# Reordering two places of a linear-attention and gated-FFN kernel: the matmuls of one of seven products, with the VectorE work around them, and the first copies of x

## Chip, cores and metric

The kernel runs on one core of a Trainium2 chip. The metric is device time in microseconds (us) of one execution; lower is better. The engines are called PE (TensorE; PEld is its loading of the stationary operand), DVE (VectorE), ACT (ScalarE), POOL (GpSimd) and SP (SyncE, which issues the DMAs).

## The reference

The input x is 2048 rows of 576. Everything is float32.

```python
xn = layernorm(x)
q, k, v = split(xn @ wqkv)                  # 32 heads of 18
pq, pk = phi(q), phi(k)                     # phi(t) = where(t > 0, t + 1, exp(t)) + 1e-6
s = ((pq @ (pk.T @ v)) / (pq . sum(pk) + 1e-6)) @ wo   # by head
h = gelu(xn @ w1 + b1)                      # 576 -> 4608
g = silu(h @ w2 + b2)                       # 4608 -> 576
out = x + s * g
```

## The kernel before

**Arithmetic.** Every float32 operand of a matmul is split into two parts that PE takes at full rate: hi is a rounded copy (made by ACT), lo is what is left, source minus hi (made by DVE; a few by POOL). A product is then three matmuls: hi by hi, hi by lo, lo by hi. A hi part of h is made at line 673, a lo part at line 676; the lo subtraction of h reads two operands from SBUF.

**Stages.** The first stage loops over 16 tiles of 128 rows: layernorm, transpose into xh and xl (lines 204 to 220), projections to k and v, and the state k.T @ v. The second stage makes q and s. The third is the FFN, whose first product (line 1119) starts at 312.4 us of the span; most of the change is there.

**The FFN.** Its loop (line 1346) has 18 steps: two halves of the rows, each with 9 chunks of four 128-wide tiles of the 4608. A step has two parts. First, two "Up" blocks (one for each pair of tiles) form xn @ w1 by a scheme of seven block products instead of eight, in the order UP = (1, 6, 7, 5, 2, 3, 4); DVE adds the products up in PSUM (lines 1009 to 1026), and ACT makes four g tiles of 128x512 by gelu (line 997) in each Up. Second, seven products (ORDER = (1, 2, 7, 4, 5, 3, 6)) form h @ w2 by the same kind of scheme. Each is done in two halves, q2 = 0 and q2 = 2; a half has two row tiles q of 128 and a PSUM bank for each, and six matmuls for each q: three for pair 0, three for pair 1 (line 1119). DVE then adds the half into the accumulator macc (line 1126). I write product (i, q2), and hi(i, pair) and lo(i, pair) for the parts of h that product i uses. CHAIN = {2: 1, 3: 5, 4: 7} says that product 2 goes on adding into the PSUM banks of product 1, 4 into those of 7, and 3 into those of 5: so PE can't start product (2, 0) before DVE has read product (1, 0) into macc, nor (4, 0) before DVE has read (7, 0).

The sources of product 1 are the g tiles as they come: (1, 0) from the first Up, (1, 1) from the second. Those of 7, 5, 6 and 3 are differences and sums that POOL makes in place (method S, lines 1073 to 1088): S(7, pair) writes the tile mid (line 1088), S(5, pair) is line 1079, S(6, pair) line 1082, S(3, pair) line 1085. S(6, 0) overwrites the source of lo(1, 0), so POOL waits for that.

**Order of the work.** The order of instructions on DVE, ACT, POOL and PE is the program's own (in_order, line 57). A step has 28 places: 0 to 6 after the products of the first Up, 7 to 13 after those of the second, 14 + 2k and 15 + 2k after the two halves of the k-th product. At each place the table PH (line 1314) issues S, hi and lo work. Places are counted after the product's own DVE and ACT work: place 11 stands behind the gelu of product 2 of the second Up and before the DVE addition of its product 3 (line 1022); place 12 behind that addition and before that of product 4 (line 1026); place 13 behind that one. Place 14 stands behind the macc addition of product (1, 0), place 15 behind that of (1, 2). The lines of PH before:

```python
lo={
    (1, 0): 10, (2, 0): 10, (1, 1): 11, (2, 1): 13, (7, 0): 14, (7, 1): 15, (4, 0): 16,
```

**The beginning.** For the first row tile (t = 0) the transposed x lies in PSUM. DVE copies k-blocks 0 and 1 to xh (line 212), ACT blocks 2 to 4 (line 213); then DVE subtracts for xl in two parts (line 217) and for the last 64 rows (line 218). The weights of k are split as they land: hi by ACT (line 260), lo by DVE or POOL (line 263). The lo parts of k-blocks 3 and 4 are both issued inside layernorm(1) (function last_lo), between its statistics and its normalization (line 186).

Of the kernel before, what the change touches and what calls it, by code (L numbers as in the profile page):

```python
# [18 lines left out]
HD = 288  # L19
# [5 lines left out]
KT = 5  # L25
# [17 lines left out]
def linear_attention_gated_ffn(ctx, tc, x, wqkv, wo, w1, w1e, b1, w2, b2, out):  # L43
    nc = tc.nc
# [35 lines left out]
    def bank2(name):  # L80
        return psum.tile([P, 2, 512], F32, tag="pp", name=name)
# [23 lines left out]
    xh, xl = {}, {}  # L105
# [52 lines left out]
    wk_h = wkvp.tile([P, KT, D], F32R, name="wk_h")  # L158
    wk_l = wkvp.tile([P, KT, D], F32R, name="wk_l")
# [5 lines left out]
    def load_x(t):  # L165
        xraw[t] = (
            stw.tile([P, D], F32, tag="stw", name=f"x{t}") if t < 2 else stage(D, f"x{t}")
        )
        nc.sync.dma_start(xraw[t], x[t * P : (t + 1) * P, :])
# [3 lines left out]
    def layernorm(t, between=lambda: None):  # L173
        st = t1.tile([P, 2, 6], F32, tag="st", name=f"st{t}")
        nc.vector.bn_stats(st[:, 0, :], xraw[t][:, :HD])
        nc.vector.bn_stats(st[:, 1, :], xraw[t][:, HD:])
        mv = t1.tile([P, 4], F32, tag="mv", name=f"mv{t}")
        nc.vector.bn_aggr(mv[:, 0:2], st)
        nc.vector.tensor_scalar_add(mv[:, 2:3], mv[:, 1:2], 1e-5)
        nc.gpsimd.tensor_tensor(mv[:, 3:4], mv[:, 2:3], nhalf, op=ALU.pow)  # L180
        stats[t] = mv
        between()
        if t < 2:
            xn[t] = t1.tile([P, 640], F32, tag="xn", name=f"xn{t}")
            for dst, src in norm_parts(t):
                nc.vector.tensor_scalar(dst, src, mv[:, 0:1], mv[:, 3:4], op0=SUB, op1=MUL)
# [8 lines left out]
    def norm_parts(t):  # L195
        return (xn[t][:, :D], xraw[t]), (xn[t][:, D:], xraw[t][:, 512:])
# [7 lines left out]
    def transpose_x(t):  # L204
        pt = bank2(f"pt{t}").rearrange("p a b -> p (a b)")
        for k in range(KT):
            nc.tensor.transpose(pt[:, k * P : (k + 1) * P], xn[t][:, k * P : (k + 1) * P], ident)
        b, c = divmod(t, 4)
        cs = slice(c * P, (c + 1) * P)
        p3 = pt[:, : KT * P].rearrange("p (k c) -> p k c", k=KT)  # L210
        if t == 0:
            nc.vector.tensor_copy(xh[b][:, :2, cs], p3[:, :2])
            nc.scalar.copy(xh[b][:, 2:, cs], p3[:, 2:])
        else:
            nc.scalar.copy(xh[b][:, :, cs], p3)  # L215
        for k in (slice(0, 2), slice(2, 4)) if t == 0 else (slice(0, 4),):
            nc.vector.tensor_tensor(xl[b][:, k, cs], p3[:, k], xh[b][:, k, cs].bitcast(F32), op=SUB)  # L217
        nc.vector.tensor_tensor(
            xh[b][64:, 4, cs], p3[64:, 4, :], xh[b][64:, 4, cs].bitcast(F32), op=SUB
        )  # L220
# [30 lines left out]
    def load_w_raw(which, k):  # L251
        if which == 2:
            raw = raw_places[k]
        else:
            raw = stage(D, f"w{which}_{k}")
        nc.sync.dma_start(raw, wqkv[k, :, which * D : (which + 1) * D])
        return raw

    def w_hi(raw, k, hi):
        nc.scalar.copy(hi[:, k, :], raw)  # L260

    def w_lo(raw, k, hi, lo, elo):
        elo.tensor_tensor(lo[:, k, :], raw, hi[:, k, :].bitcast(F32), op=SUB)

    def split_w(raw, k, hi, lo, elo):
        w_hi(raw, k, hi)
        w_lo(raw, k, hi, lo, elo)


    warm = bank1("warm")  # L270
# [159 lines left out]
    raw_k = [load_w_raw(1, k) for k in range(KT)]  # L430
    load_x(1)
    layernorm(0, lambda: split_w(raw_k[0], 0, wk_h, wk_l, nc.vector))
    split_w(raw_k[1], 1, wk_h, wk_l, nc.gpsimd)
    transpose_x(0)
    split_w(raw_k[2], 2, wk_h, wk_l, nc.gpsimd)
    for k in (3, 4):
        w_hi(raw_k[k], k, wk_h)

    def last_lo():
        for k in (3, 4):  # L440
            w_lo(raw_k[k], k, wk_h, wk_l, nc.vector)

    raw_v = [load_w_raw(2, k) for k in range(KT)]
    load_x(2)
    layernorm(1, last_lo)
    pend = None
    WQ_LOADS = {11: (0,), 12: (1, 2), 13: (3, 4)}
    WQ_SPLITS = {13: (0,), 14: (1, 2), 15: (3, 4)}
# [5 lines left out]
    for t in range(NT):  # L454
# [12 lines left out]
        if t + 1 < NT:  # L467
            if t + 1 in (8, 12):
                x_block((t + 1) // 4)
            transpose_x(t + 1)  # L470
# [225 lines left out]
    class W1:  # L696
# [39 lines left out]
        def product(self, i):  # L736

            r = we_sb[self.n][:, WE_AT[i]]
            if i == 6:
                t = self.tiles[6] if self.n < NP else six[self.n]  # L740
                return t[:, :2], t[:, 2:], r
            key, k = {1: "a0", 2: "a1", 7: "c0", 3: "c1", 5: "d0", 4: "d1"}[i]
            t, k = self.tiles[key], 2 * int(k)
            return t[:, k : k + 2], t[:, 4 + k : 6 + k], r
# [361 lines left out]
    CHAIN = {2: 1, 3: 5, 4: 7}  # L1106
    DST = {1: U1, 2: C11, 5: C22, 3: C12, 6: U1, 7: C22, 4: C21}

    def product(c, i, q2, hs, w, held):

        wh, wl = w
        ps = held.pop((CHAIN[i], q2)) if i in CHAIN else bank2(f"pm{i}")
        if i in CHAIN.values():
            held[i, q2] = ps
        for q in range(2):
            cs = slice((q2 + q) * P, (q2 + q + 1) * P)
            seq = [(st, m, p) for p in range(2) for st, m in ((0, wh), (0, wl), (1, wh))]
            for n, (st, m, p) in enumerate(seq):
                nc.tensor.matmul(  # L1119
                    ps[:, q, :HD], hs[p][st][:, cs], m[:, p, :],  # L1120
                    start=(n == 0 and i not in CHAIN), stop=(n == len(seq) - 1),
                    skip_group_check=True,
                )
        src, dst = ps[:, :, :HD], macc[:, q2 : q2 + 2, DST[i], :]
        if c > 0 or i in (5, 6):
            nc.vector.tensor_tensor(dst, src, dst, op=ADD)  # L1126
        elif i in BIAS:
            h = BIAS[i]
            bb = b2b[:, None, h * HD : (h + 1) * HD].to_broadcast([P, 2, HD])
            nc.vector.tensor_tensor(dst, src, bb, op=ADD)  # L1130
        else:
            nc.vector.tensor_copy(dst, src)
# [160 lines left out]
    def plan_w1(add, w, base, T, hi, lo):  # L1293
        for table, what in ((T, w.T), (hi, w.hi), (lo, w.lo)):
# [5 lines left out]
        hi={"a": 0, 6: 2, "c": 3, "d": 4},  # L1300
        lo={"a": 0, 6: 3, "c": 4, "d": 5},
# [3 lines left out]
        hi={"a": 6, 6: 25, "c": 26, "d": 27},  # L1305
        lo={"a": 7, 6: 25, "c": 26, "d": 27},
# [9 lines left out]
        hi={  # L1316
            (1, 0): 7, (2, 0): 9, (7, 0): 10, (1, 1): 11, (2, 1): 12, (7, 1): 15, (4, 0): 16,
            (4, 1): 17, (5, 1): 18, (5, 0): 19, (6, 0): 20, (3, 0): 21, (3, 1): 22, (6, 1): 23,
        },
        lo={  # L1320
            (1, 0): 10, (2, 0): 10, (1, 1): 11, (2, 1): 13, (7, 0): 14, (7, 1): 15, (4, 0): 16,
            (4, 1): 17, (5, 1): 18, (5, 0): 19, (6, 0): 20, (3, 0): 21, (3, 1): 22, (6, 1): 23,
        },
    )
# [18 lines left out]
    seq = ExitStack()  # L1343
    seq.enter_context(in_order(nc.vector.engine, nc.scalar.engine, nc.gpsimd.engine, nc.tensor.engine))
    n_chunks = 2 * NC
    for step in range(n_chunks):
# [78 lines left out]
        for j in range(CF // 2):  # L1425
            n = 2 * step + j
# [8 lines left out]
        for k, i in enumerate(ORDER):  # L1435
            for q2 in (0, 2):
                product(c, i, q2, [h.ops[i, 0], h.ops[i, 1]], w2t[step].ops[i], held)
                at_step(base + 14 + 2 * k + q2 // 2)
# [47 lines left out]
```

## Time and profile before

| what | value |
|---|---|
| median of 3 runs | 1125.4 us (1124.8 to 1125.44) |
| profiled execution | 1125.94 us, of which the span 1124.2 us |
| granted PE clock, mean | 0.999 |
| PE busy | 1103.8 us (98%) |
| DVE busy | 795.4 us (71%) |
| ACT busy, POOL busy | 452.4 us (40%), 451.3 us (40%) |
| time of DMA packets | 68.7% of 16 engines |

A line of the timeline reads: start, duration, engine, source line, operation, output <- input, shapes, count (consecutive like instructions are merged), and in brackets the idle time of the engine before it with what ended it. A line of the waits reads: who waited for whom, total us, times, longest us. Since matmuls are pipelined, a PE that is called busy may still lose time; the distance between starts shows it.

### The profile page before, as it was taken

The page shows a single profiled execution, that of the slowest core. Times are in us where ns is not written, and L with a number is a line of the kernel's source. Part 1 is how long each engine was busy: PE and PEld are TensorE (multiplying, and loading weights), DVE is VectorE, ACT ScalarE, POOL GpSimd, SP SyncE. Part 2 cuts the span into 40 slices and gives each one's busy share as a digit, 9 for nine tenths or more (in the row PEclk, how much of TensorE's full clock was granted, in tenths as well). Part 3 has the DMA queues.
Part 4 walks back from the last instruction along what each step waited for, and adds up shares of the span by engine and source line. Part 5 has one row for each costly group of instructions (what it writes and reads, how often), then busy time and mean ns, then how long its engine had stood idle before and what let it go on. Part 6 is the DMA issues. An engine that isn't in the chain of part 4 may idle for free. (4 is left out here: it accounts for less than half of the span.)

```text
span 1124.2 us, 18622 instructions
## 1 busy us (share of the span) xinstructions
PE 1103.8 (98%) x6972; PEld 1018.5 (91%) x6972; DVE 795.4 (71%) x1160; ACT 452.4 (40%) x772; POOL 451.3 (40%) x391
## 2 busy tenths in 40 slices
PE   8999999999999999999999999999999999999997
PEld 8999989999898988988989889898898988989987
DVE  6665448989687887877868878667475574765766
ACT  4554443333535444354443544524223242242342
POOL 4976423333344353353534523415234143242340
PEclk9999999999999999999999999999999999999999
DMA  8796832474877659467585589997777677776452
GB/s 324 264 370 254 300 137 72 160 257 157 296 248 270 239 179 342 171 242 266 181 328 193 205 302 343 315 344 242 254 233 213 206 219 215 235 211 208 131 184 85
DMA packets 84968, 264.03 MB, mean 235 GB/s; under 512 B 10381, under 2 KB 20877, under 8 KB 81295
## 3 DMA queue, kind: packets, MB, share of 16 engines
q1 hardware_dynamic: 84879, 262.85, 68.7%
q8 instruction: 55, 0.90, 0.3%
q14 instruction: 34, 0.28, 0.1%
HBM read 166.69 MB, written 94.18 MB: 232 GB/s over the span
## 5 line engine op out<-in xcount | busy, mean ns | idle before, releaser
L676 DVE TENSOR_TENSOR h_l<-g,h_h 128x512 fp32r<-128x512 f32 x204 | 174.8, 864 | 37.0 <-ACT h_h L673 21.3
L1126 DVE TENSOR_TENSOR macc<-pm,macc 128x576 f32<-128x576 f32 x218 | 163.7, 751 | 43.0 <-PE pm L1119 42.1
L673 ACT CAST h_h<-g 128x512 fp32r<-128x512 f32 x204 | 120.8, 620 | 138.1 <-PE pm L1119 137.0
L1088 POOL TENSOR_TENSOR mid<-g 128x512 f32<-128x512 f32 x34 | 43.7, 1285 | 141.0 <-ACT g L997 141.0
L1082 POOL TENSOR_TENSOR g<-g 128x512 f32<-128x512 f32 x34 | 55.1, 1621 | 56.2 <-DVE h_l L676 54.9
L997 ACT ACTIVATE g<-b,b1c 128x512 f32<-128x512 f32 x36 | 24.7, 687 | 115.8 <-DVE b L1015 115.8
L1006 ACT COPY mid<-a 128x512 f32<-128x512 f32 x36 | 21.1, 587 | 117.3 <-PE a L989 117.3
L717 POOL TENSOR_TENSOR w1raw<-w1raw 128x256 f32<-128x256 f32 x18 | 16.9, 938 | 122.5 <-DVE wa L733 122.5
L1214 POOL TENSOR_TENSOR fin1l<-fin1h,fin1l 128x288 f32<-128x288 f32 x8 | 6.5, 807 | 126.3 <-DMA fin1l<-s_dram 51.1
L1009 DVE TENSOR_TENSOR mid<-b,mid 128x512 f32<-128x512 f32 x36 | 24.7, 687 | 44.6 <-PE b L989 43.0
L1079 POOL TENSOR_TENSOR g<-g 128x512 f32<-128x512 f32 x34 | 52.2, 1535 | 2.7
L1085 POOL TENSOR_TENSOR g<-g 128x512 f32<-128x512 f32 x34 | 49.7, 1461 | 2.7
L989 PE MATMUL a<-h0r,wa 128*128 128x512 f32 x144 | 50.4, 390 | 0.0
L989 PE MATMUL a<-xh,wa 128*128 128x512 f32 x144 | 50.4, 390 | 0.0
L997 ACT ACTIVATE g<-e,b1c 128x512 f32<-128x512 f32 x36 | 24.8, 690 | 55.8 <-DVE e L1022 55.8
L1015 DVE TENSOR_TENSOR b<-e,mid 128x512 f32<-128x512 f32 x36 | 25.2, 699 | 30.3 <-PE e L989 30.3
L614 POOL TENSOR_TENSOR pbuf<-phiq,den 128x576 f32<-128x576 f32 x16 | 20.4, 1273 | 63.9 <-DVE den L613 45.1
L217 DVE TENSOR_TENSOR xl<-pt,xh 128x512 fp32r<-128x512 f32 (+1 forms) x17 | 11.1, 660 | 47.9 <-ACT xh L215 47.3
L1012 DVE TENSOR_TENSOR mid<-zy,mid 128x512 f32<-128x512 f32 x36 | 24.9, 691 | 24.6 <-PE zy L989 24.6
L311 POOL TENSOR_TENSOR w2r<-w2r 128x576 f32<-128x576 f32 x27 | 38.8, 1442 | 6.5 <-DMA w2r<-w 5.8
L1022 DVE TENSOR_TENSOR e<-e,mid 128x512 f32<-128x512 f32 x36 | 24.9, 691 | 19.8 <-PE e L989 19.8
L676 DVE TENSOR_TENSOR h_l<-mid,h_h 128x512 fp32r<-128x512 f32 x34 | 38.6, 1134 | 0.0
(810 smaller groups left out, 3617.0 us busy)
## 6 DMA issues: line engine op xcount, KB each, us to landing
we<-we_dram SPq DMA_DIRECT2D x72, 224.0 KB
op<-w2o SPq DMA_DIRECT2D x27, 576.0 KB
w2raw<-w SPq DMA_DIRECT2D x10, 1152.0 KB
w2r<-w SPq DMA_DIRECT2D x9, 1152.0 KB
w1raw<-w SPq DMA_DIRECT2D x18, 512.0 KB
op_a<-wa SPq DMA_DIRECT2D x18, 512.0 KB
op_c<-wc SPq DMA_DIRECT2D x18, 512.0 KB
op_d<-wd SPq DMA_DIRECT2D x18, 512.0 KB
```

The source lines that it names most:

```text
L311: nc.gpsimd.tensor_tensor(dst, a, b, op=SUB)
L673: nc.scalar.copy(pair[0], src)
L676: eng.tensor_tensor(pair[1], src, pair[0].bitcast(F32), op=SUB)
L989: nc.tensor.matmul(ps, st, mv, start=first and n == 0, stop=n == len(seq) - 1, skip_group_check=True,)
L997: nc.scalar.activation(g, ps, AF.Gelu_apprx_tanh, bias=b1c[:, f : f + 1])
L1012: tt(u2_sb, Z, u1_sb, op=ADD)
L1015: tt(B, E, u2_sb, op=ADD)
L1079: tt(src[5, pr], A(1, 0), A(1, 1), op=ADD)
L1082: tt(src[6, pr], src[5, pr], A(0, 0), op=SUB)
L1085: tt(src[3, pr], A(0, 1), src[6, pr], op=SUB)
L1088: tt(src[7, pr], A(0, 0), A(1, 0), op=SUB)
L1126: nc.vector.tensor_tensor(dst, src, dst, op=ADD)
```

## The change

Three edits.

1. In product 1 the matmuls that use lo(1, 1), the last of the six of each q, are issued after the other ten of the half: q = 0 numbers 0 to 4, q = 1 numbers 0 to 4, then number 5 of both. All other products keep their order.
2. In PH, lo(7, 0) goes from place 14 to place 11 and lo(1, 1) from 11 to 12. DVE's order was lo(1, 0), lo(2, 0), lo(1, 1), addition of line 1022, addition of line 1026, lo(2, 1), macc (1, 0), lo(7, 0), macc (1, 2); it becomes lo(1, 0), lo(2, 0), lo(7, 0), line 1022, lo(1, 1), line 1026, lo(2, 1), macc (1, 0), macc (1, 2).
3. At the beginning, DVE makes both copies of the first tile of x, each just ahead of the subtraction that uses it, and ACT none; the lo of k-block 3 of wk is issued ahead of layernorm(1) instead of inside it.

```diff
-        if t == 0:
-            nc.vector.tensor_copy(xh[b][:, :2, cs], p3[:, :2])
-            nc.scalar.copy(xh[b][:, 2:, cs], p3[:, 2:])
-        else:
+        if t:
             nc.scalar.copy(xh[b][:, :, cs], p3)
-        for k in (slice(0, 2), slice(2, 4)) if t == 0 else (slice(0, 4),):
+        for k, n in ((0, 2), (2, 4)) if t == 0 else ((0, 4),):
+            k, kh = slice(k, n), slice(k, KT if n == 4 else n)
+            if t == 0:
+                nc.vector.tensor_copy(xh[b][:, kh, cs], p3[:, kh])
             nc.vector.tensor_tensor(xl[b][:, k, cs], p3[:, k], xh[b][:, k, cs].bitcast(F32), op=SUB)
...
-    for k in (3, 4):
-        w_hi(raw_k[k], k, wk_h)
-
-    def last_lo():
-        for k in (3, 4):
-            w_lo(raw_k[k], k, wk_h, wk_l, nc.vector)
-
+    split_w(raw_k[3], 3, wk_h, wk_l, nc.vector)
     raw_v = [load_w_raw(2, k) for k in range(KT)]
     load_x(2)
-    layernorm(1, last_lo)
+    layernorm(1, lambda: split_w(raw_k[4], 4, wk_h, wk_l, nc.vector))
...
-        for q in range(2):
+        seq = [(st, m, p) for p in range(2) for st, m in ((0, wh), (0, wl), (1, wh))]
+        seq = [(q, n, *s) for q in range(2) for n, s in enumerate(seq)]
+        if i == 1:
+
+            seq.sort(key=lambda s: s[1] == 5)
+        for q, n, st, m, p in seq:
             cs = slice((q2 + q) * P, (q2 + q + 1) * P)
-            seq = [(st, m, p) for p in range(2) for st, m in ((0, wh), (0, wl), (1, wh))]
-            for n, (st, m, p) in enumerate(seq):
-                nc.tensor.matmul(
-                    ps[:, q, :HD], hs[p][st][:, cs], m[:, p, :],
-                    start=(n == 0 and i not in CHAIN), stop=(n == len(seq) - 1),
-                    skip_group_check=True,
-                )
+            nc.tensor.matmul(
+                ps[:, q, :HD], hs[p][st][:, cs], m[:, p, :],
+                start=(n == 0 and i not in CHAIN), stop=(n == 5), skip_group_check=True,
+            )
...
         lo={
-            (1, 0): 10, (2, 0): 10, (1, 1): 11, (2, 1): 13, (7, 0): 14, (7, 1): 15, (4, 0): 16,
+            (1, 0): 10, (2, 0): 10, (7, 0): 11, (1, 1): 12, (2, 1): 13, (7, 1): 15, (4, 0): 16,
```

The rest of the diff merges the helpers w_hi and w_lo into split_w.

More of the change, by code (lines that the diff above doesn't have):

```diff
@@ L257, in load_w_raw, with split_w @@
         return raw
-    def w_hi(raw, k, hi):
+    def split_w(raw, k, hi, lo, elo):
         nc.scalar.copy(hi[:, k, :], raw)
-    def w_lo(raw, k, hi, lo, elo):
         elo.tensor_tensor(lo[:, k, :], raw, hi[:, k, :].bitcast(F32), op=SUB)
-    def split_w(raw, k, hi, lo, elo):
-        w_hi(raw, k, hi)
-        w_lo(raw, k, hi, lo, elo)
     warm = bank1("warm")
```

## The prediction

> **What bounds the kernel now.** I read the shares of the engines first, then the waits, then the timeline of one FFN step, engine by engine.
>
> ```profile
> PE 1103.8 (98%) x6972; PEld 1018.5 (91%) x6972; DVE 795.4 (71%) x1160; ACT 452.4 (40%) x772; POOL 451.3 (40%) x391
> ```
>
> PE is the bound, so only two things can move the time: the number of matmuls, which stays the same, and the places where PE loses time between them. The waits name such a place:
>
> ```profile
> PE pm L1119 <- DVE macc L1126: 7.8, 15, 0.6
> ```
>
> Matmuls of h @ w2 wait for the macc addition, 15 times (two more, in the steps where macc is first written, go by another line: 17 steps have products). How much is lost in all, I take from the step's length, since pipelining hides part of a wait. From the chain that ended last, products without a gap and one product of the Up part:
>
> ```profile
> 1057.50 13.03 PE pm L1119 x96
> ...
> 1080.10 1.59 PE zy L989 x7
> ```
>
> 96 matmuls are eight halves of 12: about 1.60 us each (13.03 less some 0.2 us of the last one's tail, by 8). A step has 14 Up products and 14 halves: 14 x 1.59 + 14 x 1.60 = 44.7 us of work. Its real length is the distance of two equal DVE rows, 812.66 - 766.76 = 45.90 us:
>
> ```profile
> 766.76 0.70 DVE L1015 TENSOR_TENSOR b<-e,mid 128x512 f32<-128x512 f32 x1 [0.90 <-PE e L989]
> ...
> 812.66 0.70 DVE L1015 TENSOR_TENSOR b<-e,mid 128x512 f32<-128x512 f32 x1 [0.90 <-PE e L989]
> 813.27 1.28 DVE L676 TENSOR_TENSOR h_l<-g,h_h 128x512 fp32r<-128x512 f32 x2
> 815.93 1.70 DVE L676 TENSOR_TENSOR h_l<-g,h_h 128x512 fp32r<-128x512 f32 x1 [1.38 <-POOL g L1082]
> 817.55 0.69 DVE L1022 TENSOR_TENSOR e<-e,mid 128x512 f32<-128x512 f32 x1
> 818.15 0.68 DVE L1026 TENSOR_TENSOR zy<-zy,mid 128x512 f32<-128x512 f32 x1
> 819.71 0.69 DVE L676 TENSOR_TENSOR h_l<-g,h_h 128x512 fp32r<-128x512 f32 x1 [0.87 <-issue]
> 820.31 0.75 DVE L1126 TENSOR_TENSOR macc<-pm,macc 128x576 f32<-128x576 f32 x1
> 820.98 1.12 DVE L676 TENSOR_TENSOR h_l<-mid,h_h 128x512 fp32r<-128x512 f32 x1
> 822.03 0.75 DVE L1126 TENSOR_TENSOR macc<-pm,macc 128x576 f32<-128x576 f32 x1
> 822.69 1.12 DVE L676 TENSOR_TENSOR h_l<-mid,h_h 128x512 fp32r<-128x512 f32 x1
> ...
> 827.16 0.74 DVE L1126 TENSOR_TENSOR macc<-pm,macc 128x576 f32<-128x576 f32 x1
> ```
>
> So **a step loses 45.90 - 44.66 = 1.24 us, and 17 steps lose 21.1 us**, 1.9% of the time. PE's own timeline shows where:
>
> ```profile
> 815.41 0.39 PE L989 MATMUL e<-rxm,we 128*128 128x512 f32 x1
> ...
> 817.22 0.42 PE L1119 MATMUL pm<-w__8548,h_h 128*128 128x288 f32 x2
> ...
> 820.27 0.29 PE L1119 MATMUL pm<-w__8548,h_l 128*128 128x288 f32 x1
> 821.12 0.53 PE L1119 MATMUL pm<-w__8586,h_h 128*128 128x288 f32 x2 [0.55 <-DVE macc L1126]
> ...
> 828.01 0.50 PE L1119 MATMUL pm<-w__8660,h_h 128*128 128x288 f32 x2
> ```
>
> Product 1 runs from 817.22 without a gap; product (2, 0) should start at 820.40 (a matmul each 0.133 us) and starts at 821.12, right after the macc of (1, 0), in whose banks it goes on, ends at 821.06. Two halves of (2) and two of (7) later, (4, 0) starts at 828.01, after the macc of (7, 0) ends at 827.90, though 4 x 1.60 after 821.12 is 827.5: the rest of the loss.
>
> Why is the macc of (1, 0) late? Its matmuls ended by 818.9, but DVE came to it at 820.31. Backwards: lo(2, 1) waited until 819.71 for its hi; that stood behind the gelu that follows the addition of line 1022; this addition ran at 817.55, although its last matmul (the 815.41 row) ended at 815.80. In between DVE stood in lo(1, 1): 1.70 us instead of the 0.69 of the 819.71 row. POOL's timeline says why:
>
> ```profile
> 807.87 1.29 POOL L1088 TENSOR_TENSOR mid<-g 128x512 f32<-128x512 f32 x1 [4.27 <-ACT g L997]
> ...
> 814.10 1.61 POOL L1082 TENSOR_TENSOR g<-g 128x512 f32<-128x512 f32 x1 [3.56 <-DVE h_l L676]
> ...
> 815.79 1.29 POOL L1085 TENSOR_TENSOR g<-g 128x512 f32<-128x512 f32 x1
> ...
> 820.28 1.27 POOL L1088 TENSOR_TENSOR mid<-g 128x512 f32<-128x512 f32 x1 [3.20 <-ACT g L997]
> 821.64 1.63 POOL L1079 TENSOR_TENSOR g<-g 128x512 f32<-128x512 f32 x1
> 823.34 1.64 POOL L1082 TENSOR_TENSOR g<-g 128x512 f32<-128x512 f32 x1
> ```
>
> A lo part that meets a running POOL sum ends 0.55 us after that sum: 817.63 after S(3, 0) ended at 817.08, 822.10 after 821.55, 823.81 after 823.27. And a sum that meets a lo part takes 1.16 us from its end (823.81 to 824.98). The two exclude each other. The macc additions, which read PSUM, are not held up (0.75 us at 822.03, under a POOL sum). Where both wait, DVE's subtraction goes ahead of POOL's next sum (823.27, 823.34, 823.81).
>
> **The change part by part.** *Edit 2, lo(7, 0) earlier.* I replay the step of 812.66 with these durations. ACT's rows are:
>
> ```profile
> 813.98 0.61 ACT L673 CAST h_h<-mid 128x512 fp32r<-128x512 f32 x1
> ...
> 815.22 0.62 ACT L673 CAST h_h<-g 128x512 fp32r<-128x512 f32 x1
> ...
> 819.00 0.62 ACT L673 CAST h_h<-g 128x512 fp32r<-128x512 f32 x1
> 819.52 0.68 ACT L997 ACTIVATE g<-zy,b1c 128x512 f32<-128x512 f32 x1
> ...
> 821.59 0.63 ACT L673 CAST h_h<-mid 128x512 fp32r<-128x512 f32 x1 [1.39 <-POOL mid L1088]
> ```
>
> hi(7, 0) is ready at 814.59. lo(7, 0) comes after lo(2, 0), finds S(6, 0) running until 815.71 and ends at 816.26. Queued behind it are the additions of lines 1022 and 1026, and PE, ACT and POOL through them; but line 1022 could not start before 815.80 anyway. It now ends at about 816.9, 1.3 us earlier than before, since the subtraction ahead of it waits for the first sum instead of the second. S(3, 0) runs from 816.26 to 817.42; lo(1, 1), issued at 816.85, its hi ready at 815.84, ends at 817.97. Line 1026 follows, until 818.57 (818.83 before). hi(2, 1) is ready at 818.2 and lo(2, 1) ends at 819.15. The macc of (1, 0), its matmuls done by 818.9, ends at 819.8, **1.2 us earlier and 0.6 ahead of (2, 0)**. The macc of (1, 2) follows at once after PE, until 821.2, ahead of (2, 2) at 822.0. So both gaps of product 2 go.
>
> What is late next is product (4, 0). The last gelu starts at 818.61 instead of 819.52, so S(7, 1) ends at 820.66; S(5, 1), with no lo(7, 0) in its way, at 822.0. lo(7, 1) then ends at 822.57 (823.81 before), and the alternation of lo and sum goes on in rounds of 1.71 us as before: lo(4, 0) at 824.28, lo(4, 1) at 826.0, the macc of (7, 0) at 826.67. PE, without gaps, wants it at 817.22 + 6 x 1.60 = 826.8, less 0.13 for loading the stationary operand. That is level: I allow 0.06 us a step, with ends of 0 and 0.3 (in the first nine steps POOL also has sums for w1 behind these, which may catch one more lo).
>
> *Edit 1, the matmuls.* Their number and operands are the same. lo(1, 1), which ends at 817.97 instead of 817.63, was wanted by the sixth matmul at 817.22 + 5 x 0.133 = 817.89: without this edit the later place would cost some 0.1 to 0.3 us. As the eleventh it is wanted at 818.55, less 0.13; 0.45 us are to spare. Changing banks three times instead of once in a half is not in the trace except as the change from q = 0 to q = 1, which shows no gap; I take nothing, between 0 and 0.1 us a step.
>
> *Edit 3, the beginning.*
>
> ```profile
> 7.14 0.42 DVE L212 CAST xh<-pt 128x256 fp32r<-128x256 f32 x1 [0.64 <-PE pt L207]
> 8.11 0.76 DVE L217 TENSOR_TENSOR xl<-pt,xh 128x256 fp32r<-128x256 f32 x2 [0.55 <-ACT xh L213]
> ...
> 9.84 0.46 DVE L175 BATCH_NORM_STATS2 st<-x 128x6 f32<-128x288 f32 x1 [0.65 <-DMA x<-x]
> ...
> 11.02 1.43 DVE L263 TENSOR_TENSOR wk_l<-w,wk_h 128x576 fp32r<-128x576 f32 x2
> 12.36 0.80 DVE L186 TENSOR_SCALAR xn<-x,mv 128x576 f32<-128x576 f32 x2
> ```
>
> ```profile
> 11.17 1.02 POOL L180 TENSOR_TENSOR mv<-mv,nhalf 128x1 f32<-128x1 f32 x1 [0.89 <-DVE mv L179]
> ```
>
> DVE no longer idles 0.55 us for ACT's copy, but makes one of 384 columns itself (0.42 us for 256; about 0.55): the subtractions end when they did, the first of them some 0.5 us sooner. The lo of block 3, half of 1.43 us, moves into the 0.65 us that DVE waits for x. That saves DVE 0.7 us inside layernorm(1); but the normalization at 12.36 also waits for POOL's power, which started at 11.17 and sat behind one such subtraction, and one is still there. So PE's next transposes come when they did: 0, with ends of -0.4 (all of DVE's gain) and +0.3 (statistics pushed behind the lo).
>
> *Sum.* 17 x (1.24 - 0.06) = 20.1 us off. The profiled execution, 1125.94, becomes 1105.8; the median, 0.54 less, 1125.4 - 20.1 = **1105.3**.
>
> The Trainium skill (SBUF — State Buffer, Who interferes with whom) says that a DVE instruction with two SBUF inputs and a POOL instruction that reads SBUF take a shared port pair as an exclusive lock, whichever starts first, the other fully blocked. The 1.70 us of lo(1, 1) agree. It does not say who goes first when both wait at a release; read in POOL's favour, it leads to the first rival below, 1119 instead of 1105.3.
>
> **The rivals.** *POOL goes first.* lo(7, 0) waits through S(3, 0) too and ends at 817.63, where lo(1, 1) did. Line 1022 stays at 817.55, lo(1, 1) ends at 818.85, 0.45 late even for the eleventh matmul; the macc of (1, 0) ends at 821.0 as before, and only the alternation after S(7, 1) is 0.3 us earlier. PE loses about 0.4 in product 1, 0.25 at (2, 0), 0.2 at (4, 0): 0.87 a step, a gain of 17 x 0.37 = 6.3 us, **1119**. Against it stand the three orders above, for it that none of them is at this place.
>
> *The gap at (4, 0) stays.* The alternation of lo and POOL sums is as slow as before, and if other subtractions meet it, 0.3 to 0.6 us a step remain: 17 x 0.8 = 14 us off, about **1112**.
>
> *Slower: POOL's finishing work holds lo(7, 0).* In the second half POOL also finishes output rows, in its queue ahead of S(7, 0):
>
> ```profile
> 1031.97 0.81 POOL L1215 TENSOR_TENSOR fin3l<-fin3l,fin4h 128x288 f32<-128x288 f32 x1
> ...
> 1037.38 1.29 POOL L1088 TENSOR_TENSOR mid<-g 128x512 f32<-128x512 f32 x1 [4.61 <-ACT g L997]
> ```
>
> It waits for DMAs. Before, a late S(7, 0) reached lo(7, 0) at place 14; now at place 11 it would stop lines 1022 and 1026 and with them PE, microsecond for microsecond. It takes hold when the DMAs land 4.6 us later than here (the idle time of the second row) and some 4.8 more, the distance from S(7, 0)'s end at 809.16 in the replayed step to ACT's use at 813.98. With 8 such steps, 20 us are eaten when each is 2.5 us beyond that; at 4 us beyond, 12 us are lost on balance: **1137**. Nothing in the trace is that late.
>
> **How the numbers follow.** The forecast has 0.72 (its own range 1103.5 to 1108.5: the residues above, and edit 3's ends), the gap that stays 0.10, POOL first 0.12, slower 0.05; 0.01 for no change. A measurement can tell about 0.2% (2.3 us). The two partial cases are faster by more than that, unless they come out far smaller than worked out (0.02): faster 0.92, same 0.03, slower 0.05. The range takes in the forecast with all gaps gone (1125.4 - 21.1 - 0.4 = 1103.9, less 0.6 for rounding of the step's work) and the gap that stays with its bounds: 1103.3 to 1114.
>
> **What would show it.** Right: steps of about 44.7 us between rows of line 1015; the wait of pm for macc gone at (2, 0); lo(7, 0) about 1.6 us long and directly behind the pair of lo parts; line 1022 at 3.5 us after line 1015 instead of 4.9; a rest of the gap, if any, at (4, 0). Wrong: lo(7, 0) longer than 2.5 us (POOL first), PE waiting at the eleventh matmul of product 1, or steps of the second half longer than those of the first.

## The result, and the profile after

The changed kernel took 1106.94 us (median of 4 runs, 1106.3 to 1108.02) beside 1125.42 us for the kernel before: a ratio of 0.9835, 95% interval 0.9818 to 0.9852, 18.5 us less. The profiled execution went from 1125.94 to 1106.44 us. The forecast was 1105.3 us. Two single executions among the experiments below lie far out, 1540.53 us with edit 1 alone (clock 0.654) and 2797.16 us with edit 3 alone, and the medians and ratios are those of the others.

The page of the changed kernel, its span and its engines:

```profile
span 1104.7 us, 18604 instructions
...
PE 1093.5 (99%) x6972; PEld 1017.6 (92%) x6972; DVE 799.0 (72%) x1161; ACT 454.9 (41%) x771; POOL 451.6 (41%) x391
```

The same matmuls take 10.3 us less busy time, because PE's busy time had covered part of the waits. What DVE, ACT and POOL do is unchanged to within 4 us: one copy went from ACT to DVE (edit 3), and otherwise only the order differs. Among the waits, the one of pm for the macc addition (7.8 us, 15 times before) is gone, and so is its twin at line 1132 (1.0 us, twice); what is left of PE's waits on pm is

```profile
PE pm L1110 <- ACT h_h L661: 0.2, 1, 0.2
PE pm L1110 <- DVE h_l L664: 0.2, 1, 0.2
```

once each (lines are 9 to 12 lower in the changed kernel: 664 is the lo subtraction, 1003, 1010 and 1014 are the additions in PSUM that were 1015, 1022 and 1026, 1116 is macc). The step replayed in the prediction, on DVE and then on POOL; its times are 12.06 us earlier than there (800.60 against 812.66):

```profile
800.60 0.70 DVE L1003 TENSOR_TENSOR b<-e,mid 128x512 f32<-128x512 f32 x1 [0.89 <-PE e L977]
801.21 1.28 DVE L664 TENSOR_TENSOR h_l<-g,h_h 128x512 fp32r<-128x512 f32 x2
802.56 1.63 DVE L664 TENSOR_TENSOR h_l<-mid,h_h 128x512 fp32r<-128x512 f32 x1
804.12 0.69 DVE L1010 TENSOR_TENSOR e<-e,mid 128x512 f32<-128x512 f32 x1
804.72 1.18 DVE L664 TENSOR_TENSOR h_l<-g,h_h 128x512 fp32r<-128x512 f32 x1
805.82 0.69 DVE L1014 TENSOR_TENSOR zy<-zy,mid 128x512 f32<-128x512 f32 x1
806.42 0.68 DVE L664 TENSOR_TENSOR h_l<-g,h_h 128x512 fp32r<-128x512 f32 x1
807.02 0.75 DVE L1116 TENSOR_TENSOR macc<-pm,macc 128x576 f32<-128x576 f32 x1
808.54 0.76 DVE L1116 TENSOR_TENSOR macc<-pm,macc 128x576 f32<-128x576 f32 x1 [0.78 <-PE pm L1110]
809.29 1.24 DVE L664 TENSOR_TENSOR h_l<-mid,h_h 128x512 fp32r<-128x512 f32 x1
...
813.86 0.74 DVE L1116 TENSOR_TENSOR macc<-pm,macc 128x576 f32<-128x576 f32 x1
```

```profile
802.03 1.61 POOL L1070 TENSOR_TENSOR g<-g 128x512 f32<-128x512 f32 x1 [3.56 <-DVE h_l L664]
803.72 1.62 POOL L1073 TENSOR_TENSOR g<-g 128x512 f32<-128x512 f32 x1
...
807.31 1.29 POOL L1076 TENSOR_TENSOR mid<-g 128x512 f32<-128x512 f32 x1 [1.96 <-ACT g L985]
808.67 1.30 POOL L1067 TENSOR_TENSOR g<-g 128x512 f32<-128x512 f32 x1
```

lo(7, 0), the 802.56 row, waits for S(6, 0) and ends at 804.19; S(3, 0) is now the sum that waits (1.62 us instead of 1.29); line 1010 runs 3.52 us after line 1003 instead of 4.89; and DVE stands idle for 0.78 us ahead of the macc of (1, 2), where it had been behind before. PE, in the same step:

```profile
805.16 0.42 PE L1110 MATMUL pm<-w__8548,h_h 128*128 128x288 f32 x2
...
808.35 0.43 PE L1110 MATMUL pm<-w__8586,h_h 128*128 128x288 f32 x2
...
814.75 0.47 PE L1110 MATMUL pm<-w__8660,h_h 128*128 128x288 f32 x2
...
849.84 0.42 PE L1110 MATMUL pm<-w__8989,h_h 128*128 128x288 f32 x2
```

Product (2, 0) starts 3.19 us after product 1 (3.90 before), (4, 0) 6.40 us later, and the next step's product 1 44.68 us after this one's (45.9 before). Of the 16 distances between the first products of two steps, 15 are 44.64 to 44.68 us. One, around 760 us, is 45.55; it comes back below.

### The profile page after: what moved, and what is told of

The parts are those of the page before. It is cut to its first block, busy times and chain, and to the rows that moved or that the text cites. A ratio compares the mean times of both kernels' runs of the same rounds, so it can differ in the third digit from the quotient of the medians.

```text
span 1104.7 us, 18604 instructions
## 1 busy us (share of the span) xinstructions
PE 1093.5 (99%) x6972; PEld 1017.6 (92%) x6972; DVE 799.0 (72%) x1161; ACT 454.9 (41%) x771; POOL 451.6 (41%) x391
## 4 chain that ended last, share of the span: by engine, by line
PE 96%; DVE 2%; ACT 0%; issue 0%; DMA 0%; POOL 0%; SPq 0%; DVEq 0%; ACTq 0%
PE pm L1110 34%; PE a L977 10%; PE e L977 10%; PE zy L977 10%; PE pv L236 5%; PE b L977 5%; PE pk L236 5%; PE pq L236 5%; PE ps_s L637 5%; PE pd L1229 2%; PE ps_kva L273 1%; PE pt L207 1%; PE ptp L619 1%; PE ps_kw L565 1%; DVE h_l L664 0%
## 5 line engine op out<-in xcount | busy, mean ns | idle before, releaser
L664 DVE TENSOR_TENSOR h_l<-g,h_h 128x512 fp32r<-128x512 f32 x204 | 165.9, 820 | 0.0
L664 DVE TENSOR_TENSOR h_l<-mid,h_h 128x512 fp32r<-128x512 f32 x34 | 48.8, 1436 | 1.6 <-ACT h_h L661 0.4
```

The costliest lines, as they stand in the source:

```text
L664: eng.tensor_tensor(pair[1], src, pair[0].bitcast(F32), op=SUB)
```

## The experiments

Ten programs were run, the first of them the changed kernel itself. The FFN's steps are compared by the distance of their first product matmuls, since that doesn't depend on the beginning.

**The changed kernel again.** No edit.

> The changed kernel once more, as the measure for the other three. The step length between the starts of two product parts should be 44.67 us in all steps but those in which POOL's finishing of output rows comes late; in the first look one of 17 steps was 0.88 us longer. If that lateness varies from run to run, as a late DMA would, one to three steps are longer and the time lies between 1106 and 1108; if it is fixed by the program, it is the same step by the same 0.9 us again.

Measured: 1106.35 us against 1127.11 for the kernel before, measured beside it, ratio 0.9819 (0.9804 to 0.9834). 15 distances are 44.66 to 44.68 us, one is 45.37, the same one. So it is the same step both times, and its extra length varies: 0.88 and 0.70 us. (With half of edit 3 taken back, below, the step is 44.71 us, hardly longer than the others.)

**Edit 1 alone.**

```diff
...
+        if i == 1:
+            seq.sort(key=lambda s: s[1] == 5)
...
```

> Edit 1 alone: lo(1, 1) is used by the last two matmuls of each half of product 1, the lo order as before. Theory: product 1 had no gap, so nothing is gained, and changing banks three times instead of once costs nothing: steps 45.9 us, 1125.4 within 1. Rival: the matmul order is what frees the step: 1106 to 1110.

Measured: 1125.85 us against 1126.16, ratio 0.9999 (0.9989 to 1.0009); distances 45.87 to 45.91 us but for one of 45.41. The order of the matmuls by itself gains nothing and costs nothing. A step that waits for DVE could hide a small cost on PE, so for the bank changes the time of the half says more: product (1, 2) starts 1.59 us after (1, 0) here, as in the kernel before.

**Edit 2 alone.**

```diff
-            (1, 0): 10, (2, 0): 10, (1, 1): 11, (2, 1): 13, (7, 0): 14, (7, 1): 15, (4, 0): 16,
+            (1, 0): 10, (2, 0): 10, (7, 0): 11, (1, 1): 12, (2, 1): 13, (7, 1): 15, (4, 0): 16,
```

> Edit 2 alone: lo(7, 0) and lo(1, 1) in the new places, matmuls of product 1 in the old order. Theory: lo(1, 1) ends 0.74 us after product 1's start (805.90 against 805.16 in the changed kernel), the sixth matmul wants it at 0.67 less 0.13 for its stationary load, so PE loses 0.15 to 0.3 us in each step there and nothing elsewhere: steps of about 44.9 us, 17 x 0.2 = 3 to 4 us above the changed kernel, about 1110. Rival: edit 1 does the work and edit 2 little: steps near 45.9 us, 1123 to 1126. Second rival: edit 1 is worth nothing: 1106 to 1107.

Measured: 1109.86 us against 1127.11, ratio 0.9848 (0.9833 to 0.9863); distances 44.88 to 44.90 us but for one of 46.10. The lo order makes nearly the whole gain. What is lost without edit 1 is at the sixth matmul of product 1, as the timelines of DVE and PE show:

```profile
356.48 1.17 DVE L676 TENSOR_TENSOR h_l<-g,h_h 128x512 fp32r<-128x512 f32 x1
```

```profile
356.92 0.42 PE L1119 MATMUL pm<-w__4114,h_h 128*128 128x288 f32 x2
...
357.71 0.40 PE L1119 MATMUL pm<-w__4114,h_l 128*128 128x288 f32 x1
```

lo(1, 1) ends at 357.65, and the matmul that uses it starts at 357.71 instead of 357.58. With its follower that is 0.23 us a step: 44.89 against 44.66.

**Edits 1 and 2 without 3.** The changed kernel with the beginning of before.

> Edits 1 and 2 without edit 3 (the beginning as before). Theory: the whole gain is in the FFN steps, and the beginning of the changed kernel costs 0.2 to 0.6 us: the first product of the FFN starts near 312.4 us as before (313.0 in the changed kernel), steps are 44.67 us, and the time is 0.2 to 0.6 us below the changed kernel, about 1106.4. Rival: the later start is only a later landing of the first weights, which has nothing to do with edit 3; then the first product's start agrees with the changed kernel's within the jitter of that landing, and so does the time.

Measured: 1107.52 us against 1127.11, ratio 0.9824 (0.9807 to 0.9841), not to be told from the changed kernel's. The first product starts at 311.80 us instead of 312.93, so the beginning is earlier by more than was expected; 0.5 of these 1.1 us are DVE's first copy, which comes at 7.19 instead of 7.70 us. In the profiled execution the gain was eaten in the steps: three distances are 45.25, 45.30 and 46.46 us, and PE's waits in them are

```profile
703.21 0.47 PE L989 MATMUL a<-h0r,wa 128*128 128x512 f32 x1 [0.34 <-DMA wa<-op_a]
```

```profile
734.17 0.50 PE L1122 MATMUL pm<-w__8005,h_h 128*128 128x288 f32 x2 [0.40 <-DMA w__8005<-op]
```

```profile
762.29 0.40 PE L1122 MATMUL pm<-w__8107,h_l 128*128 128x288 f32 x1 [1.11 <-DVE h_l L676]
```

Around the change from the first to the second half two DMAs were late for PE by 0.3 and 0.4 us in this execution; the same two steps are 44.66 or 44.67 us in both executions of the changed kernel. The finishing step loses 1.8 us.

**Edit 3 alone.** Only the beginning of the changed kernel.

> Edit 3 alone: only the beginning is changed. Theory: steps stay 45.9 us; the transposes of the second row tile come 0.2 to 0.6 us later, since the lo of k-block 3 now stands in front of the statistics of the second tile and itself waits for POOL's lo of block 2; time 1125.6 to 1126.0, not to be told from 1125.4. Rival: DVE's own copies save the 0.55 us that it waited for ACT, and the transposes come earlier: 1124.9.

Measured: 1127.17 us against 1127.11, ratio 1.0004 (0.9995 to 1.0014); distances 45.88 to 45.91 us. The first product starts at 313.42 us. From DVE's first copy (8.16) to the normalization of the second tile (13.38) it takes 5.22 us; in the two kernels above with the beginning of before it is 4.61 (7.19 to 11.80, edits 1 and 2) and 4.60 (8.06 to 12.66, edit 1). All five kernels with the old beginning that were run as experiments lie between 4.6 and 4.75.

**One half of edit 3 taken back.**

```diff
-    split_w(raw_k[3], 3, wk_h, wk_l, nc.vector)
+    for k in (3, 4):
+        nc.scalar.copy(wk_h[:, k, :], raw_k[k])
+    def last_lo():
+        for k in (3, 4):
+            nc.vector.tensor_tensor(
+                wk_l[:, k, :], raw_k[k], wk_h[:, k, :].bitcast(F32), op=SUB
+            )
...
-    layernorm(1, lambda: split_w(raw_k[4], 4, wk_h, wk_l, nc.vector))
+    layernorm(1, last_lo)
```

> The changed kernel with the lo parts of wk's k-blocks 3 and 4 both inside layernorm(1) again, as before the change; DVE's two copies of the first tile stay. It splits edit 3. Theory: what the edit costs is the lo of block 3 ahead of the statistics of the second tile. From DVE's first copy to its normalization of that tile, 4.6 us were measured without edit 3 (7.19 to 11.80) and 5.2 with it (7.70 to 12.92); here 4.6 to 4.7. The time is that of the changed kernel less some 0.6 us, 1105 to 1107, not to be told from it by the times alone. Rival: DVE's second copy costs as much: 5.2 again.

Measured: 1105.75 us (five runs, 1105.08 to 1111.91) against 1126.91, ratio 0.9831 (0.9808 to 0.9854). DVE at the beginning, first of the changed kernel, then of this one:

```profile
7.55 0.42 DVE L216 CAST xh<-pt 128x256 fp32r<-128x256 f32 x1 [0.64 <-PE pt L207]
...
9.71 0.97 DVE L261 TENSOR_TENSOR wk_l<-w,wk_h 128x576 fp32r<-128x576 f32 x1
...
10.61 0.45 DVE L175 BATCH_NORM_STATS2 st<-x 128x6 f32<-128x288 f32 x1
...
11.77 0.76 DVE L261 TENSOR_TENSOR wk_l<-w,wk_h 128x576 fp32r<-128x576 f32 x1
12.98 0.81 DVE L186 TENSOR_SCALAR xn<-x,mv 128x576 f32<-128x576 f32 x2 [0.45 <-POOL mv L180]
```

```profile
7.73 0.42 DVE L216 CAST xh<-pt 128x256 fp32r<-128x256 f32 x1 [1.06 <-PE pt L207]
...
9.91 0.46 DVE L175 BATCH_NORM_STATS2 st<-x 128x6 f32<-128x288 f32 x1
...
12.44 0.80 DVE L186 TENSOR_SCALAR xn<-x,mv 128x576 f32<-128x576 f32 x2
```

From the copy to the normalization it is 4.71 us, and 5.43 in the changed kernel. So the lo ahead of the statistics costs 0.5 to 0.7 us, and the copies on DVE 0.1 at most. This is the lowest median of the ten, but its interval covers the changed kernel's; only the trace tells the two apart.

**S(3, 0) behind S(7, 1).** The kernel before with one of POOL's places changed; nothing of DVE or PE is touched.

```diff
-        S={..., (6, 0): 11, (3, 0): 11, (7, 1): 13, (5, 1): 14, ...},
+        S={..., (6, 0): 11, (7, 1): 13, (3, 0): 13, (5, 1): 14, ...},
```

> The kernel before with one POOL place changed: S(3, 0) is issued behind S(7, 1) instead of ahead of it; DVE's order and the matmuls are those of before. Theory: what holds the step is that lo(1, 1) runs into this POOL sum; without it lo(1, 1) takes 0.69 us instead of 1.70, the addition of line 1022 comes more than 1 us earlier, the macc of (1, 0) is in time and steps are 44.7 us: about 1106, as after the whole change, and 1112 at most if the sum then delays the alternation behind it. Rival: DVE's order alone counts (lo(7, 0) between two macc additions, lo(1, 1) ahead of line 1022): no change, 1125.

Measured: 1113.66 us against 1126.16, ratio 0.9886 (0.987 to 0.9902). lo(1, 1) and line 1022 in this kernel (line 1015 started at 804.37), and the macc of (7, 0), on DVE:

```profile
807.63 0.69 DVE L676 TENSOR_TENSOR h_l<-g,h_h 128x512 fp32r<-128x512 f32 x1 [1.37 <-POOL g L1082]
808.24 0.69 DVE L1022 TENSOR_TENSOR e<-e,mid 128x512 f32<-128x512 f32 x1
...
817.86 0.74 DVE L1126 TENSOR_TENSOR macc<-pm,macc 128x576 f32<-128x576 f32 x1
```

With the sum out of its way, lo(1, 1) takes 0.69 us instead of 1.70 and line 1022 comes at 3.87 us instead of 4.89; the gap at (2, 0) is gone. But the sum now stands in the alternation of lo parts and sums: the macc of (7, 0) ends at 818.60, and (4, 0) starts late at 818.71, 9.78 us after product 1 instead of 9.59 in the changed kernel. Distances are 45.25 us in the first half and 45.0 in the second. The mechanism is as the theory has it, but its upper bound of 1112 was passed: the rest that stays was larger than I had worked out (0.3 to 0.6 us a step).

**lo(7, 0) at place 12, lo(1, 1) left at 11.**

```diff
-            (1, 0): 10, (2, 0): 10, (1, 1): 11, (2, 1): 13, (7, 0): 14, (7, 1): 15, (4, 0): 16,
+            (1, 0): 10, (2, 0): 10, (1, 1): 11, (7, 0): 12, (2, 1): 13, (7, 1): 15, (4, 0): 16,
```

> The kernel before with lo(7, 0) moved to place 12, behind line 1022, and lo(1, 1) left at place 11, ahead of it. So lo(7, 0) is out from between the macc additions, but lo(1, 1) still meets S(3, 0). Theory: the first gap, at (2, 0), stays (0.8 us), those at (2, 2) and (4, 0) go: steps of 45.5 us, 1125.4 - 17 x 0.38 = 1119. Rival: taking lo(7, 0) away from behind the macc of (1, 0) is the whole gain: 44.7 us, 1106.

Measured: 1120.58 us against 1126.16, ratio 0.9945 (0.9928 to 0.9962); distances 45.55 to 45.60 us but for one of 46.36. PE still waits at (2, 0):

```profile
361.26 0.40 PE L1119 MATMUL pm<-w__4133,h_h 128*128 128x288 f32 x1 [0.49 <-DVE macc L1126]
```

So taking lo(7, 0) from behind the macc addition is worth 0.33 us a step, about a quarter of the 1.23. Edit 2 as a whole is worth 1.01 (44.89), so by difference 0.68 come with lo(1, 1) no longer holding line 1022, and edit 1 adds 0.23. The 0.33 us show at S(5, 1), which no longer meets lo(7, 0) and takes 1.29 us instead of 1.63; the macc of (7, 0) and with it (4, 0), 10.44 us after product 1 instead of 10.79, come as much earlier. (2, 0) is late by 0.65 us still.

**lo(1, 1) directly behind lo(7, 0).** The changed kernel, one place changed.

```diff
-            (1, 0): 10, (2, 0): 10, (7, 0): 11, (1, 1): 12, (2, 1): 13, (7, 1): 15, (4, 0): 16,
+            (1, 0): 10, (2, 0): 10, (7, 0): 11, (1, 1): 11, (2, 1): 13, (7, 1): 15, (4, 0): 16,
```

> The changed kernel with lo(1, 1) directly behind lo(7, 0), ahead of line 1022 instead of behind it. It tells who goes first when DVE has its next subtraction ready as the last one ends and POOL's S(3, 0) waits too. If DVE keeps the way: lo(1, 1) takes 0.7 us, S(3, 0) follows it, steps stay 44.67 us, 1106 to 1107. If POOL gets it: lo(1, 1) takes 1.7 us and holds line 1022 up by as much, the macc of (1, 0) ends about 0.8 us later than in the changed kernel, steps of 44.9 to 45.1 us, 1111 to 1114.

Measured: 1126.90 us against 1126.16, ratio 1.0005 (0.9996 to 1.0015). The swap of two neighbours on DVE, lo(1, 1) and line 1010, takes the whole gain away, more than either theory said. DVE, POOL and PE (the macc row is that of (7, 0), the last PE row is (4, 0)):

```profile
814.58 0.70 DVE L1003 TENSOR_TENSOR b<-e,mid 128x512 f32<-128x512 f32 x1 [0.89 <-PE e L977]
...
816.54 1.64 DVE L664 TENSOR_TENSOR h_l<-mid,h_h 128x512 fp32r<-128x512 f32 x1
818.10 1.78 DVE L664 TENSOR_TENSOR h_l<-g,h_h 128x512 fp32r<-128x512 f32 x1
819.80 0.69 DVE L1010 TENSOR_TENSOR e<-e,mid 128x512 f32<-128x512 f32 x1
...
829.07 0.74 DVE L1116 TENSOR_TENSOR macc<-pm,macc 128x576 f32<-128x576 f32 x1
```

```profile
816.01 1.62 POOL L1070 TENSOR_TENSOR g<-g 128x512 f32<-128x512 f32 x1 [3.56 <-DVE h_l L664]
817.71 1.62 POOL L1073 TENSOR_TENSOR g<-g 128x512 f32<-128x512 f32 x1
...
823.88 1.31 POOL L1067 TENSOR_TENSOR g<-g 128x512 f32<-128x512 f32 x1
```

```profile
819.14 0.43 PE L1110 MATMUL pm<-w__8548,h_h 128*128 128x288 f32 x2
...
823.31 0.53 PE L1110 MATMUL pm<-w__8586,h_h 128*128 128x288 f32 x2 [0.82 <-DVE macc L1116]
...
829.91 0.50 PE L1110 MATMUL pm<-w__8660,h_h 128*128 128x288 f32 x2
```

lo(7, 0) ends at 818.18. lo(1, 1) is next on DVE and its hi has been ready since 817.75, but S(3, 0) runs first, until 819.33, and lo(1, 1) ends 0.55 us after it. DVE now stands behind both sums: line 1010 comes at 5.22 us after line 1003 (4.89 in the kernel before), and (2, 0) starts 4.17 us after product 1 (3.90 before, 3.19 after the change). The first gap is larger than in the kernel before, and yet the steps are equally long, because it is (4, 0) that sets them. The macc of (7, 0) starts 14.49 us after line 1003 here and 14.50 after line 1015 before: what S(3, 0) costs more (1.62 us instead of 1.29), S(5, 1), with no lo(7, 0) in its way, gives back (1.31 instead of 1.63). (4, 0) starts 10.77 us after product 1 here, 10.79 before, 10.44 with lo(7, 0) at place 12 and 9.59 after the change, and the steps are 45.90, 45.90, 45.57 and 44.67 us: they follow it, and not the gap at (2, 0) that the waits name.

**Without the finishing of one tile.** The changed kernel; `1 <= c` becomes `2 <= c` where the finishing work is issued.

> The changed kernel without the finishing of output rows 1024 to 1151: their loads, POOL's four operations and the two stores are left out of the second step of the second half, so these rows of the output are not written. Theory: the 0.88 us by which that step was longer come from POOL's finishing work, which arrives late, holds S(7, 0) and S(5, 0), and through lo(1, 0) and lo(7, 0) everything behind on DVE: without it this step is 44.67 us like the others, and the profiled execution 0.9 us shorter, about 1105.6. Rival: the step is longer for another reason, such as the loads of the second half's operands: it stays at 45.5 us.

Measured: 1106.26 us in one run; all 16 distances are 44.65 to 44.67 us, the finishing step's too. In the changed kernel POOL has, in that step,

```profile
750.68 0.81 POOL L1204 TENSOR_TENSOR fin1l<-fin1h,fin1l 128x288 f32<-128x288 f32 x1 [27.51 <-DMA fin1l<-s_dram]
...
753.23 0.81 POOL L1205 TENSOR_TENSOR fin3l<-fin3l,fin4h 128x288 f32<-128x288 f32 x1
754.00 1.29 POOL L1076 TENSOR_TENSOR mid<-g 128x512 f32<-128x512 f32 x1
755.37 1.29 POOL L1067 TENSOR_TENSOR g<-g 128x512 f32<-128x512 f32 x1
```

and on DVE the pair of lo(1, 0) and lo(2, 0) meets S(5, 0) and takes 2.15 us instead of 1.28. Counted from product 1, S(5, 0) starts 3.7 us later than in the kernel without the finishing (4.24 us ahead of it instead of 7.98). PE feels it at the eleventh matmul of product 1, and once more at (4, 0):

```profile
755.66 2.15 DVE L664 TENSOR_TENSOR h_l<-g,h_h 128x512 fp32r<-128x512 f32 x2
757.74 1.78 DVE L664 TENSOR_TENSOR h_l<-mid,h_h 128x512 fp32r<-128x512 f32 x1
...
760.04 1.18 DVE L664 TENSOR_TENSOR h_l<-g,h_h 128x512 fp32r<-128x512 f32 x1
```

```profile
761.27 0.53 PE L1110 MATMUL pm<-w__8107,h_l 128*128 128x288 f32 x2 [0.18 <-DVE h_l L664]
```

So that step's 0.88 us come from the finishing work. One execution without it would not show this alone, since with half of edit 3 taken back the step is 44.71 us with the finishing in it. But there POOL ended its finishing 38.27 us after the product 1 of the step before, S(5, 0) was over early enough, and the pair of lo parts took 1.30 us. The later that end, the longer the step: 38.93 us and 0.70 us more, 39.10 and 0.88, 40.95 and 1.8 (edits 1 and 2 without 3, where the pair took 3.11 us). The profiled span is 0.9 us shorter than the changed kernel's (1103.8 against 1104.7), although its first product came 0.4 later (313.41 instead of 313.00); the profiled time is only 0.2 us less, since 2.5 us of it lie outside the span instead of 1.7.

## Why the prediction was right, point by point

- **The size of the loss** (1.24 us a step, 21.1 us in 17 steps) was right: gapless steps are 44.67 us long (forecast 44.7), and 17 x (45.90 - 44.67) = 20.9 us.
- **The replay of the step** was right to 0.03 us in the rows that matter. With 12.06 us taken off: lo(7, 0) was to end at 804.20 and ended at 804.19; line 1010 at 804.84 (804.81); lo(1, 1) at 805.91 (805.90); line 1014 at 806.51 (806.51); S(7, 1) at 808.60 (808.60); lo(7, 1) at 810.51 (810.53); the macc of (7, 0) at 814.61 (814.60). It could be replayed because DVE, ACT and POOL have a fixed order and durations that repeat, once the exclusion of DVE's lo parts and POOL's sums is put in. Only the macc of (1, 2) came later than said, by 0.16 us (809.30 against 809.14), where there was time to spare.
- **The cause** is shown by undoing: moving POOL's sum alone brings 12.5 us (1113.66), and putting lo(1, 1) back in the sum's way takes everything away (1126.90). The prediction put most of the loss at (2, 0) and only the rest at (4, 0). The experiments show that (4, 0) sets the step of the kernel before: a gap at (2, 0) that is 0.27 us longer leaves it at 45.90. The prediction came out right all the same, since it followed both things that hang on the late line 1022: the macc of (1, 0) and, by the last gelu and S(7, 1), the macc of (7, 0).
- **Edit 1** was priced at 0.1 to 0.3 us a step in the presence of edit 2: 0.23 measured. Its bank changes were taken at nothing: right (the half is 1.59 us long as before).
- **The residue at (4, 0)**, taken at 0.06 us a step, is below 0.05: the macc of (7, 0) ends at 814.60 and (4, 0) starts at 814.75.
- **Edit 3** was mis-sized: 0 forecast, with ends of -0.4 and +0.3; 0.5 to 0.7 us measured. The step that failed is that the lo of block 3 "moves into the 0.65 us that DVE waits for x". That wait belonged to the one profiled execution. In the five kernels run later with the beginning of before, DVE idles 0.03 to 0.17 us ahead of the statistics, so the lo is in the chain.
- **The slower rival** had the right origin, but neither its way nor its price. POOL's finishing work does reach PE, in one step, for 0.04 to 1.8 us. It doesn't do so by a late S(7, 0) that holds lo(7, 0), as forecast: hi(7, 0) was ready at 756.99, before DVE came to lo(7, 0) at 757.74. It does so by S(5, 0) running into lo(1, 0), which stands where it stood. With lo(7, 0) at place 12, behind line 1022, that step is 0.8 us longer as well (46.36 us). I had left the loss out of the likeliest case, because the slack that I measured was that of another step (around 1032 us). In the step that matters, S(7, 0) had no idle time ahead of it in the trace of before either (759.01 to 763.60 was all finishing work and S(7, 0)).
- **The sum.** For the profiled execution: 20.9 off, 0.9 back in the finishing step, 0.6 back at the beginning, gives 19.4; measured 19.5. Of the 0.6, 0.4 is DVE's first copy, at 7.55 us instead of 7.14; it lies between 7.18 and 8.06 in the five kernels with the old beginning, so this pair can't put it down to edit 3. The median came out 1.6 us above the forecast. The two terms make 1.5 of it; that 20.9 us came off the steps instead of 20.1 takes 0.8 back; the remaining 1.0 is where the profiled executions happen to lie, 0.5 above the median before and 0.5 below it after.

The first rival, that POOL goes first, was wrong where I had put it: lo(7, 0) went ahead of S(3, 0) at the end of S(6, 0). But the evidence that I had quoted for DVE's precedence holds only for the end of a POOL sum. At the end of a DVE subtraction it is the other way round (819.33 in the kernel with lo(1, 1) directly behind).

What stays open: the finishing step's extra length, 0.04 to 1.8 us, was traced to when POOL ends the finishing work, and that to DMAs that land late (the idle time ahead of 750.68); why they land when they do wasn't tried.

## What to carry to other kernels

When an in-order engine is late at a place that matters, follow its queue backwards to the first instruction that took longer than its equals, and ask what ran beside it; here a subtraction of 0.69 us took 1.70, some 3 us and four instructions ahead of the wait that the profile named. Then ask which of the late places ends the step: here it was (4, 0), and the wait listed at (2, 0) could grow by 0.27 us at no cost. An instruction that can be blocked belongs behind those that others wait for, even if it is itself needed soon, and the consumer's order can be bent to give it time. Don't fill an idle time that only one execution shows: look whether it is a wait for something that varies, such as a DMA's landing.

## What the runs showed of the hardware

DVE's subtraction with two operands in SBUF and POOL's sum exclude each other, and where both are ready the turn changes: at the end of a POOL sum the waiting subtraction goes (ending 0.55 us later), at the end of a subtraction the waiting sum goes (1.16 us), even if DVE's next subtraction is ready and directly behind. So two such subtractions in a row, with two sums waiting, cost the second one a whole sum: 1.78 us instead of 0.69. The Trainium skill (SBUF — State Buffer, Who interferes with whom) says that issue order decides who blocks. The trace agrees as far as it goes: S(3, 0) is on record from 817.71, the subtraction that it blocks only from 818.10. That the change of turns follows from this order is my reading; no run here tests it.

Additions that read PSUM are not held up: the macc addition takes 0.74 to 0.76 us with and without a sum beside it.
